# Splitting the qkv weight sums by tile, other interleaving constants, and a last product in two column halves, in a fused attention and GLU kernel on one Trainium2 core

## The chip, the core and the metric

The kernel runs on one core of a Trainium2 chip. The core has a matrix engine (TensorE; PE in the profile for its matmuls, PEld for its weight loads), VectorE (DVE), ScalarE (ACT), GpSimd (POOL) and SyncE (SP), each with its own instruction queue that is worked through in order, and 16 DMA engines that SP, ACT and POOL give transfers to. Matmuls write PSUM, which is divided into eight banks of 128 partitions by 512 f32; everything else lies in SBUF, 128 partitions wide. The metric is the device time of one execution in microseconds.

## What is computed

A sliding-window attention (32 heads of 32, eight keys per query at distances 0, 2, ..., 14) and a gated feed-forward layer work on the same 2048 rows of 1024, and a sigmoid gate per row mixes them. All inputs and outputs are bf16.

```python
def reference(A_x, A_wqkv, A_wo, B_x, B_w_gate, B_w_up, B_w_down, gate_w):
    x = A_x                                                   # 1 x 2048 x 1024
    g = sigmoid((x * gate_w).sum(-1, keepdims=True))
    # attention: q, k, v = x @ wqkv (1024 x 3072); softmax over 8 keys
    #   s, s-2, ..., s-14 of each head; o @ wo (1024 x 1024)
    a = _A_ref(x, A_wqkv, A_wo)
    # feed-forward: (gelu(x @ w_gate) * (x @ w_up)) @ w_down, 1024 -> 3584 -> 1024
    b = _B_ref(x, B_w_gate, B_w_up, B_w_down)
    return g * a + (1 - g) * b
```

## The kernel before, in words

**Tiling.** The rows are worked on in four chunks `c` of 512 (`SC`), in two pairs (`sup` 0: chunks 0 and 1; `sup` 1: chunks 2 and 3). Each large product is done as a 2x2 block product in Strassen's way with seven multiplications instead of eight, for which sums and differences of weight blocks, of activations and of partial results are needed. TensorE does the multiplications as matmuls of 128x128 weights with 512 moving columns. VectorE makes the sums, and with ScalarE it empties the banks.

**Stages of TensorE**, in the order of `main()`: turning the first rows, the q product of the first pair (`first_pair`, L592, and L772), k and v of the first pair (`qkv_pair`, L772), the feed-forward products of the first pair (`ffn`, L1136) with the beginning of the output product of chunk 0 in them (`down`, L1305), the rest of that output product, q, k and v of the second pair (L592, L772; in the order q, v, k, `QVK`), the output product of chunk 1, the feed-forward products of the second pair, and the output products of chunks 2 and 3. The last thing that is computed is the seventh multiplication (`m` = 6) for the second half (`g` = 1) of chunk 3: 18 matmuls into one bank, which ScalarE scales into an SBUF tile (`scaled`, L1346) and SP writes to DRAM (`evac`, L1338).

**VectorE's other work.** In the gaps between the sums it does the attention of all chunks: products of queries and shifted keys (L937) and their additions (L943), the softmax (L1014 to L1060), products with values (L1084) and additions (L1094, L1098, L1102). In the products of q, k and v it empties banks: in `qkv_pair` at L837, by an addition that must be done before the bank's last product (T4, the form `(1, 1)`) may start, and at L847; in `ffn` at L1203 and L1224.

**The weight sums at L709** (`qkv_forms`). For each of q, k and v of a pair, four sums `f` are made, each in two operations `kt` = 0 and 2, and each operation covers two neighbouring weight tiles `kt` and `kt + 1`. The raw tiles (128 x 1024 each) lie, for most of them, in slots of a ring of 20 (`ring`, one slot of 128 x 1024 for each tile); the slots are handed out in the order in which they come free, so two neighbouring tiles need not be neighbours. The operand of an operation is therefore written with the distance between the two slots as its outermost step. `f` = 2 is made in place in the raw tiles; the others take a slot of the ring.

**What sets the order.** `Weave.run` takes operations from eleven streams (main line, loads, sums, preparation of `w_down` and `wo` forms, attention, scores and so on) and issues the one that its own clock thinks can start first. To that start time each stream's bias is added, unless the operation has a due time that is near; an operation may have a bias of its own. The bias of the streams, the due times `DUE`, and the costs of the operations are constants in the source. The order on each engine is fixed when the program is built; waits are by semaphore.

Of the kernel before, what the change touches and what calls it, by code (L numbers as in the profile page):

```python
# [9 lines left out]
ALU = mybir.AluOpType  # L10
# [17 lines left out]
def _win_ap(src: bass.AP, dims):  # L28
    return AP(src.tensor, src.offset, [list(src.ap[0])] + [list(d) for d in dims])
# [125 lines left out]
def kernel(  # L155
# [68 lines left out]
    DUE = (77.1, 303.05)  # L224
# [25 lines left out]
    def dve(cost, fn, deps=(), **kw):  # L250
        return Op("DVE", cost, fn, deps, **kw)
# [211 lines left out]
    def preps():  # L463
        for i0 in range(0, NPREP, 2):
# [5 lines left out]
            f0 = dve(t, lambda: V(out=b11, in0=b12, in1=b11, op=ALU.subtract), due=DUE[0] + 3.05 * i0, deps=[("prep", i0), ], lag=1.0)  # L470
            yield f0
            yield dve(t, lambda: V(out=b12, in0=b22, in1=b12, op=ALU.subtract), due=DUE[0] + 3.05 * i0)
            f1 = dve(t, lambda: V(out=b22, in0=b22, in1=b11, op=ALU.subtract), [f0], due=DUE[0] + 3.05 * i0)
            yield f1
            last = dve(t, lambda: V(out=b21, in0=b21, in1=b22, op=ALU.subtract), [f1], due=DUE[0] + 3.05 * i0)
# [12 lines left out]
    def wforms():  # L488
        t = tt(GR)
        for b in range(NBLK):  # L490
            ops = []
            for f, x_, y_, op in ((0, "U21", "A22", ALU.add), (2, "A11", "U21", ALU.subtract), (1, 0, "A11", ALU.subtract),
                                  (3, "A12", 1, ALU.subtract)):
                def go(f=f, x_=x_, y_=y_, op=op, b=b):
# [4 lines left out]
                        due=DUE[0] + 12.1 * b)  # L499
# [187 lines left out]
    def qkv_forms():  # L687
        for sup in range(NSUP):
            c = 2 * sup
            t = tt(D)  # L690
            for which in QVK if sup else (0, 1, 2):
                def raw(kt, hi, which=which, c=c):
                    w0, w1 = qkv_w(c, which, kt), qkv_w(c, which, kt + 1)
                    return _win_ap(w0[:, KH * hi:KH * hi + 1], [[w1.offset - w0.offset, 2], [NT, P], [1, KH]])

                def form(f, kt, which=which, c=c):
                    return ring[:, held["wqf", c, which, f, kt // 2], :].rearrange("p (k m t) -> p k m t", k=2, t=KH)

                for f in range(4):
                    for kt in range(0, KH, 2):  # L700
                        def go(f=f, kt=kt, which=which, c=c):
# [7 lines left out]
                            V(out=o(), in0=x_(), in1=y_(), op=op)  # L709
# [574 lines left out]
    def down(c):  # L1284
# [5 lines left out]
        def prod(bk, m, g, start, deps):  # L1290
# [7 lines left out]
            for q in range(last + 1):  # L1298
                def fn(q=q):
                    wv = piece(("wd", c, m, q), 2)  # L1300
                    for i in range(2):
                        k = 2 * q + i
                        l, kk = (ops[g][a][0], k) if k < FH else (ops[g][a][1], k - FH)
                        l = l[:, kk // 2, kk % 2, :] if len(l.shape) == 4 else l[:, kk, :]
                        nc.tensor.matmul(banks[bk][:], lhsT=l, rhs=wv[:, i, :], start=(start and k == 0),  # L1305
                                         stop=(q == last and i == 1), skip_group_check=True)
# [3 lines left out]
                if g == 1:  # L1310
                    ring_give(("wd", c, m, q), o)
# [18 lines left out]
    def down_rest(c, prod, ev, A, Bk, Dk, m5, u2, omg, steps):  # L1330
# [4 lines left out]
        def evac(e_op, j, nh, ost):  # L1335
            yield e_op
            yield Op("SP" if last else "POOL", (P * NW * 2, 0.5),
                     lambda: eng.dma_start(out=o2[s0 + j * P:s0 + (j + 1) * P, nh * NW:(nh + 1) * NW], in_=ost[0]),  # L1338
                     [e_op])
# [8 lines left out]
        for m, g in steps:  # L1348
# [3 lines left out]
            if True:  # L1352
# [25 lines left out]
                elif m == 4:  # L1378
# [4 lines left out]
                    yield from evac(ev[g, "x"], j2, 1, box)  # L1383
                elif m == 5:
# [5 lines left out]
                    bank_give(Dk[g], e)  # L1390
                else:
# [7 lines left out]
    def main():  # L1399
# [57 lines left out]
```

## Time and profile before

| What | Value |
|---|---|
| Median of three runs | 722.49 us (722.13 to 722.61) |
| The profiled execution, span from the first to the last instruction | 720.1 us |
| What lies around that span, by the median | 2.4 us |
| Granted TensorE clock over the span | 1.000 |
| DMA moved over the span | 176.84 MB, mean 246 GB/s |
| VectorE busy, 84 to 251 us | 163.3 of 167 us |
| VectorE busy, 251 to 309 us | 51.2 of 58 us |
| VectorE busy, 309 to 344 us | 34.7 of 35 us |
| VectorE busy, 344 to 384 us | 32.5 of 40 us |
| VectorE busy, 384 to 616 us | 211.1 of 232 us |
| L709 in all | 48 operations of 128x1024, 678 to 694 ns each |

The profiled execution's span is measured on the core; a run's time also holds what comes before the first and after the last instruction. In the tables that follow, times are microseconds from the span's start. A line of the timeline gives the start, the length, the engine, the line of the source, the operation, its output and inputs, how many instructions were put together (x), and in square brackets how long the engine had been idle before and what ended that. The length of an operation is from its start to its end; on VectorE and ScalarE the next operation can begin some 0.08 us before that end, when it needs nothing from it. On TensorE the end of a matmul is modelled, and the next one starts well before it: rows of matmuls start 0.216 us apart.

### The profile page before, as it was taken

The numbers are of one execution on the slowest core, as the hardware profiler recorded it, in microseconds if no ns is written. First come the engines' busy times: TensorE is split into PE (matmuls) and PEld (weight loads), VectorE is DVE, ScalarE is ACT, GpSimd is POOL, SyncE is SP. The second block draws the span as 40 slices with busy tenths as digits, with TensorE's granted clock in tenths as the row PEclk, the third lists the DMA queues.
The fourth block names the chain that finished last, engine by engine and source line by source line (L and its number), as shares of the span: only waits on it lengthen the run. The fifth ranks groups of instructions, "written<-read, shape, count | busy, mean of one in ns | idle before, by whom it ended". The sixth has DMA issues, their size and how long they took to land.

```text
span 720.1 us, 9892 instructions
## 1 busy us (share of the span) xinstructions
PE 710.1 (99%) x3337; PEld 342.7 (48%) x3337; DVE 609.8 (85%) x862; ACT 323.8 (45%) x547; POOL 73.8 (10%) x130
## 2 busy tenths in 40 slices
PE   7999999999999999999999999999999999999997
PEld 3556544444444444456554444444444444444443
DVE  4989999999998999799789988799999997849300
ACT  3354585555585522153465323258556655310110
POOL 0020333343121100100000000100000000001000
PEclk9999999999999999999999999999999999999999
DMA  9953899996797799943378899996647656999992
GB/s 263 363 192 97 248 295 311 362 317 225 179 249 230 238 253 330 336 174 117 88 214 272 277 299 352 311 310 186 185 137 194 172 165 161 322 294 376 297 338 93
DMA packets 184179, 176.84 MB, mean 246 GB/s; under 512 B 58304, under 2 KB 140224, under 8 KB 184000
## 3 DMA queue, kind: packets, MB, share of 16 engines
q1 hardware_dynamic: 174512, 145.53, 68.6%
q0 software_dynamic: 9328, 30.42, 11.6%
q8 instruction: 26, 0.43, 0.2%
q10 hardware_dynamic: 288, 0.26, 0.1%
q14 instruction: 25, 0.20, 0.1%
HBM read 132.12 MB, written 31.46 MB: 227 GB/s over the span
## 4 chain that ended last, share of the span: by engine, by line
PE 96%; DVE 1%; SPq 1%; DMA 1%; issue 0%; ACT 0%; DVEq 0%
PE ps L1136 47%; PE ps L1305 30%; PE ps L772 18%; PE ps L592 1%; SPq L357 1%; DMA hT<-in_A_wqkv_dram 1%; DVE ring L709 0%; SPq L428 0%; DVE lend L837 0%; DVE tf L518 0%; DVE zt L880 0%; PE ps L874 0%; ACT ost L1346 0%; DVE hT L709 0%; PE ps L898 0%
## 5 line engine op out<-in xcount | busy, mean ns | idle before, releaser
L1136 PEld LDWEIGHTS <-ring 128*128 128x128 bf16 x1568 | 153.2, 98 | 185.1 <-issue 0.5
L1136 PE MATMUL ps<-lend,ring 128*128 128x512 bf16 x896 | 212.7, 379 | 0.0
L1136 PE MATMUL ps<-tf,ring 128*128 128x512 bf16 x672 | 164.3, 379 | 0.0
L1305 PE MATMUL ps<-ring,hT 128*128 128x512 bf16 x708 | 160.7, 379 | 0.0
L1305 PEld LDWEIGHTS <-hT 128*128 128x128 bf16 x708 | 69.1, 98 | 83.8 <-DVE ost L1380 0.4
L1084 DVE TENSOR_TENSOR xbuf<-xbuf,lend 128x2048 bf16<-128x2048 bf16 x64 | 77.5, 1217 | 16.6 <-DMA xbuf<-xbuf 16.5
L772 PEld LDWEIGHTS <-ring 128*128 128x128 bf16 x512 | 65.0, 127 | 49.6 <-issue 3.6
L937 DVE TENSOR_TENSOR xbuf<-qo,lend 128x2048 bf16<-128x2048 bf16 x64 | 77.0, 1218 | 2.3 <-ACT lend L830 2.3
L943 DVE TENSOR_TENSOR xbuf<-xbuf 128x2048 bf16<-128x2048 bf16 x56 | 68.2, 1218 | 0.2
L772 PE MATMUL ps<-tf,ring 128*128 128x512 bf16 x256 | 58.4, 380 | 3.2 <-DVE lend L837 1.4
L772 PE MATMUL ps<-lend,ring 128*128 128x512 bf16 x256 | 57.9, 379 | 0.0
L1346 ACT ACTIVATE ost<-ps,omg 128x512 bf16<-128x512 f32 x16 | 11.0, 687 | 101.3 <-PE ps L1305 89.7
L1168 ACT COPY ps<-ps 128x512 f32<-128x512 f32 x56 | 32.1, 573 | 51.8 <-PE ps L1136 51.6
L1212 ACT ACTIVATE gl<-ps 128x512 bf16<-128x512 f32 x56 | 33.5, 598 | 46.5 <-PE ps L1136 46.3
L1305 PE MATMUL ps<-ring,qo 128*128 128x512 bf16 x192 | 49.3, 380 | 0.0
L1338 POOL DMA_DIRECT2D out_dram<-ost x24 | 13.0, 541 | 336.6 <-ACT ost L1346 248.3
L1185 DVE TENSOR_TENSOR hT<-hT,gl 128x1024 bf16<-128x1024 bf16 x56 | 38.3, 685 | 8.6 <-ACT hT L1178 8.5
L505 POOL DMA_DIRECT2D fforms<-ring x56 | 30.8, 551 | 144.2 <-DVE ring L496 138.1
L1224 DVE TENSOR_TENSOR u<-ps,u 128x512 f32<-128x512 f32 x56 | 38.3, 685 | 2.7 <-PE ps L1136 2.3
L1228 ACT ACTIVATE gl<-u 128x512 bf16<-128x512 f32 x56 | 35.4, 633 | 11.3 <-DVE u L1224 10.7
L1220 ACT COPY u<-ps 128x512 f32<-128x512 f32 x56 | 32.8, 586 | 14.3 <-PE ps L1136 14.3
L1094 DVE TENSOR_TENSOR xbuf<-xbuf 128x2048 bf16<-128x2048 bf16 x32 | 38.9, 1217 | 0.1
(120 smaller groups left out, 668.8 us busy)
## 6 DMA issues: line engine op xcount, KB each, us to landing
ring<-dforms SPq DMA_DIRECT2D x112, 256.0 KB, 5.0
ring<-in_B_w_down_dram SPq DMA_DIRECT2D x84, 256.0 KB, 5.4
ring<-in_B_w_gate_dram SPq DMA_DIRECT2D x56, 256.0 KB, 5.4
fforms<-ring POOLq DMA_DIRECT2D x56, 256.0 KB, 5.2
ring<-fforms SPq DMA_DIRECT2D x56, 256.0 KB, 4.1
ring<-in_B_w_up_dram SPq DMA_DIRECT2D x42, 256.0 KB, 4.8
ring<-in_A_wqkv_dram SPq DMA_DIRECT2D x32, 256.0 KB, 4.5
ring<-oforms SPq DMA_DIRECT2D x32, 256.0 KB, 5.6
```

What stands on the lines that cost most here:

```text
L772: nc.tensor.matmul(banks[bk][:], lhsT=lhsT, rhs=rhs[:, kt, :], start=(start and kt == 0), stop=(kt == KH - 1), skip_group_check=True)
L937: V(out=w3(box[t]), in0=q_b, in1=k_w, op=ALU.mult)
L943: V(out=w3(box[0]), in0=w3(box[0]), in1=w3(box[t]), op=ALU.add)
L1084: return dve(tt(n), taking(("p", t), lambda: V(out=w3(box["p", t]), in0=w3(box["ab"]), in1=v_w, op=ALU.mult)), [("qkv", c, 2, t), abo] + ( ...
L1094: V(out=p0.rearrange("p (u n) -> p u n", u=2), in0=lo, in1=hi, op=ALU.add)
L1136: nc.tensor.matmul(banks[bk][:], lhsT=wv[:, k, fl * P:(fl + 1) * P], rhs=rhs[:, k, :], start=(start and k == 0), stop=(k == KH - 1), skip_ ...
L1185: yield dve(tt(2 * SC), lambda hv=hv, gv=gv: nc.vector.tensor_tensor(out=hv, in0=hv, in1=gv, op=ALU.mult), [e, ev[f, "g1"], ev[f, "g2"]], ...
L1212: nc.scalar.activation(out=gl[f][:, r1 * SC:(r1 + 1) * SC], in_=banks[A[f]][:], func=ACT.Gelu_apprx_tanh)
L1220: nc.scalar.copy(out=u2[f][:], in_=banks[Bk[f]][:])
L1224: e = dve(tt(SC, True), lambda f=f: nc.vector.tensor_tensor(out=u2[f][:], in0=banks[Dk[f]][:], in1=u2[f][:], op=ALU.add), [o, ev[f, "u2"]])
L1228: ev[f, "g2"] = act(0.54, lambda f=f: nc.scalar.activation(out=gl[f][:, r2 * SC:(r2 + 1) * SC], in_=u2[f][:], func=ACT.Gelu_apprx_tanh), [ ...
L1305: nc.tensor.matmul(banks[bk][:], lhsT=l, rhs=wv[:, i, :], start=(start and k == 0), stop=(q == last and i == 1), skip_group_check=True)
```

## The change

Four things are done.

**The sums at L709.** When the slots of the two tiles are neighbours, an operation stays as it was. Otherwise it is written as two operations, one for each tile, of half the size. This holds for an operation as soon as one of its raw operands lies apart. The planner is told 0.065 us more for each operation whose raw tiles lie in the ring.

**Constants.** The due times of the `w_down` and `wo` preparations, of the feed-forward weight sums and of the qkv sums, the operations' own bias for the first pair's q and k sums, and the bias of five streams.

**The last product.** The multiplication `m` = 6, `g` = 1 of chunk 3 is done as two passes of 18 matmuls with 256 columns each, where it was 18 matmuls with 512. The second pass goes into another bank, into which ScalarE copies the upper 256 columns of the accumulated bank after the fifth multiplication (`m` = 4) has been taken out. Each pass is scaled by ScalarE and written to DRAM by itself.

**The output write** (`evac`) takes a range of columns.

```diff
-    DUE = (77.1, 303.05)
+    DUE = (80.01, 302.59)
...
-            f0 = dve(t, lambda: V(out=b11, in0=b12, in1=b11, op=ALU.subtract), due=DUE[0] + 3.05 * i0, deps=[("prep", i0), ], lag=1.0)
+            f0 = dve(t, lambda: V(out=b11, in0=b12, in1=b11, op=ALU.subtract), due=DUE[0] + 2.82 * i0, deps=[("prep", i0), ], lag=1.0)
...
-                        due=DUE[0] + 12.1 * b)
+                        due=DUE[0] + 11.2 * b)
...
                 def raw(kt, hi, which=which, c=c):
                     w0, w1 = qkv_w(c, which, kt), qkv_w(c, which, kt + 1)
-                    return _win_ap(w0[:, KH * hi:KH * hi + 1], [[w1.offset - w0.offset, 2], [NT, P], [1, KH]])
+                    step = w1.offset - w0.offset
+                    if step == D:
+                        return [_win_ap(w0[:, KH * hi:KH * hi + 1], [[D, 2], [NT, P], [1, KH]])]
+                    return [_win_ap(z[:, KH * hi:KH * hi + 1], [[NT, P], [1, KH]]) for z in (w0, w1)]
...
+                def parts(z, n):
+                    return z if len(z) == n else [z[0][:, k] for k in range(2)]
...
-                            V(out=o(), in0=x_(), in1=y_(), op=op)
+                            args = [z() for z in (o, x_, y_)]
+                            m = max(len(z) for z in args)
+                            for o1, x1, y1 in zip(*[parts(z, m) for z in args]):
+                                V(out=o1, in0=x1, in1=y1, op=op)
...
-                        op = dve(t, go, dep, key=("wq", c, which, f, kt), lag=0.5,
+                        op = dve(t if c < 2 and which != 1 else t + 0.065, go, dep, key=("wq", c, which, f, kt), lag=0.5,
...
-                                 bias=(0.1, -0.6)[which == 0] if which < 2 and not sup else None,
-                                 due=DUE[1] + 23.0 * QVK.index(which) + 2.5 * f if sup else 0.0)
+                                 bias=(0.19, -1.0)[which == 0] if which < 2 and not sup else None,
+                                 due=DUE[1] + 12.84 * QVK.index(which) + 0.09 * f if sup else 0.0)
...
+                    if last and g == 1:
+                        hi, fr = bank_take(True)
+                        ev["hi"] = act(0.3, lambda g=g: nc.scalar.copy(out=banks[hi][:, 0:NW // 2], in_=banks[Bk[g]][:, NW // 2:NW]),
+                                       [ev[g, "x"]] + ([fr] if fr else []), after=True)
+                        yield ev["hi"]
...
+                elif last and g == 1:
+                    hw = NW // 2
+                    o = yield from prod(Bk[g], m, g, False, [ev[g, "x"]], (0, hw))
+                    e = act(0.4, lambda g=g, om2=om2, box=box: nc.scalar.activation(
+                        out=ost_tile(box)[:, 0:hw], in_=banks[Bk[g]][:, 0:hw], func=ACT.Copy, scale=om2), [o])
+                    yield from evac(e, j2, 0, box, 0, hw)
+                    bank_give(Bk[g], e)
+                    o = yield from prod(hi, m, g, False, [ev["hi"]], (hw, NW))
+                    e = act(0.4, lambda om2=om2, box=box: nc.scalar.activation(
+                        out=box[0][:, hw:NW], in_=banks[hi][:, 0:hw], func=ACT.Copy, scale=om2), [o])
+                    yield from evac(e, j2, 0, box, hw, NW)
+                    bank_give(hi, e)
...
-    w.run([(0.0, main()), (0.0, loads()), (0.0, late_x()), (0.0, moves(3)), (0.63, wforms()), (0.0, down_forms()), (0.1, x_forms()), (2.39, qkv_forms()),
-           (2.06, preps()), (0.02, attention()), (0.28, scores())])
+    w.run([(0.0, main()), (0.0, loads()), (0.0, late_x()), (0.0, moves(3)), (0.64, wforms()), (0.0, down_forms()), (0, x_forms()), (2.0, qkv_forms()),
+           (1.54, preps()), (0.1, attention()), (0.28, scores())])
```

`prod` and `evac` get the column range as arguments (`cols`, `o0` and `c0`, `c1`); for all other products they are called as before.

More of the change, by code (lines that the diff above doesn't have):

```diff
@@ L469, in preps @@
             t = tt(n * NW)
-            f0 = dve(t, lambda: V(out=b11, in0=b12, in1=b11, op=ALU.subtract), due=DUE[0] + 3.05 * i0, deps=[("prep", i0), ], lag=1.0)
+            f0 = dve(t, lambda: V(out=b11, in0=b12, in1=b11, op=ALU.subtract), due=DUE[0] + 2.82 * i0, deps=[("prep", i0), ], lag=1.0)
             yield f0
-            yield dve(t, lambda: V(out=b12, in0=b22, in1=b12, op=ALU.subtract), due=DUE[0] + 3.05 * i0)
-            f1 = dve(t, lambda: V(out=b22, in0=b22, in1=b11, op=ALU.subtract), [f0], due=DUE[0] + 3.05 * i0)
+            yield dve(t, lambda: V(out=b12, in0=b22, in1=b12, op=ALU.subtract), due=DUE[0] + 2.82 * i0)
+            f1 = dve(t, lambda: V(out=b22, in0=b22, in1=b11, op=ALU.subtract), [f0], due=DUE[0] + 2.82 * i0)
             yield f1
-            last = dve(t, lambda: V(out=b21, in0=b21, in1=b22, op=ALU.subtract), [f1], due=DUE[0] + 3.05 * i0)
+            last = dve(t, lambda: V(out=b21, in0=b21, in1=b22, op=ALU.subtract), [f1], due=DUE[0] + 2.82 * i0)
             yield last
@@ L693, in raw @@
                     w0, w1 = qkv_w(c, which, kt), qkv_w(c, which, kt + 1)
-                    return _win_ap(w0[:, KH * hi:KH * hi + 1], [[w1.offset - w0.offset, 2], [NT, P], [1, KH]])
+                    step = w1.offset - w0.offset
+                    if step == D:
+                        return [_win_ap(w0[:, KH * hi:KH * hi + 1], [[D, 2], [NT, P], [1, KH]])]
+                    return [_win_ap(z[:, KH * hi:KH * hi + 1], [[NT, P], [1, KH]]) for z in (w0, w1)]
                 def form(f, kt, which=which, c=c):
-                    return ring[:, held["wqf", c, which, f, kt // 2], :].rearrange("p (k m t) -> p k m t", k=2, t=KH)
+                    return [ring[:, held["wqf", c, which, f, kt // 2], :].rearrange("p (k m t) -> p k m t", k=2, t=KH)]
+                def parts(z, n):
+                    return z if len(z) == n else [z[0][:, k] for k in range(2)]
                 for f in range(4):
@@ L1288, in down, with prod @@
         A, Bk, Dk, m5, u2, ev = {}, {}, {}, {}, {}, {}
-        def prod(bk, m, g, start, deps):
+        def prod(bk, m, g, start, deps, cols=(0, NW), o0=0):
             a = SEQ[m][0]
@@ L1304, in fn @@
                         l = l[:, kk // 2, kk % 2, :] if len(l.shape) == 4 else l[:, kk, :]
-                        nc.tensor.matmul(banks[bk][:], lhsT=l, rhs=wv[:, i, :], start=(start and k == 0),
-                                         stop=(q == last and i == 1), skip_group_check=True)
+                        nc.tensor.matmul(banks[bk][:, o0:o0 + cols[1] - cols[0]], lhsT=l, rhs=wv[:, i, cols[0]:cols[1]],
+                                         start=(start and k == 0), stop=(q == last and i == 1), skip_group_check=True)
                 need = [("h", sup, FH + 2 * q + 1)] if (m == 1 and 2 * q < FH) else []
@@ L1309, in prod @@
                 yield o
-                if g == 1:
+                if g == 1 and cols[1] == NW:
                     ring_give(("wd", c, m, q), o)
@@ L1333, in down_rest, with evac @@
         eng = nc.sync if last else nc.gpsimd
-        def evac(e_op, j, nh, ost):
+        def evac(e_op, j, nh, ost, c0=0, c1=NW):
             yield e_op
-            yield Op("SP" if last else "POOL", (P * NW * 2, 0.5),
-                     lambda: eng.dma_start(out=o2[s0 + j * P:s0 + (j + 1) * P, nh * NW:(nh + 1) * NW], in_=ost[0]),
+            yield Op("SP" if last else "POOL", (P * (c1 - c0) * 2, 0.5),
+                     lambda: eng.dma_start(out=o2[s0 + j * P:s0 + (j + 1) * P, nh * NW + c0:nh * NW + c1], in_=ost[0][:, c0:c1]),
                      [e_op])
```

## The prediction

> **What bounds the kernel now.** First the page's busy times and the shares of the chain that ended last.
>
> ```profile
> PE 710.1 (99%) x3337; PEld 342.7 (48%) x3337; DVE 609.8 (85%) x862; ACT 323.8 (45%) x547; POOL 73.8 (10%) x130
> ...
> PE 96%; DVE 1%; SPq 1%; DMA 1%; issue 0%; ACT 0%; DVEq 0%
> ```
>
> TensorE sets the end. Nothing can be won but its waits, its own work and the tail behind it. So next the waits of TensorE (total, times, longest):
>
> ```profile
> PE ps L592 <- DMA hT<-in_A_wqkv_dram: 1.5, 1, 1.5
> PE ps L772 <- DVE lend L837: 1.4, 2, 0.9
> PE ps L772 <- DVE tf L516: 1.0, 1, 1.0
> PE ps L322 <- DVE xbuf L320: 0.9, 1, 0.9
> PE ps L772 <- DVE zt L880: 0.8, 1, 0.8
> PE ps L592 <- ACT lend L559: 0.7, 1, 0.7
> ```
>
> All but L837 fall before 21 us. The two waits for L837, in TensorE's timeline:
>
> ```profile
> 338.21 5.34 PE L772 MATMUL ps<-lend,ring 128*128 128x512 bf16 x24
> 344.50 1.89 PE L772 MATMUL ps<-tf,ring 128*128 128x512 bf16 x8 [0.94 <-DVE lend L837]
> ...
> 363.49 5.34 PE L772 MATMUL ps<-lend,ring 128*128 128x512 bf16 x24
> 369.27 1.89 PE L772 MATMUL ps<-tf,ring 128*128 128x512 bf16 x8 [0.44 <-DVE lend L837]
> ```
>
> The idle time shown is too small for what is lost, since a matmul's modelled end lies after the next one could start. By the start distance (the output products run 468 matmuls in 101.02 us in the chain, 0.216 each), 24 matmuls from 338.21 let the next start at 343.39; it started at 344.50: 1.11 lost. From 363.49: 368.67 against 369.27, 0.60 lost. VectorE's timeline says why L837 is late:
>
> ```profile
> 308.65 5.21 DVE L709 TENSOR_TENSOR ring<-ring 128x1024 bf16<-128x1024 bf16 x8 [1.07 <-DMA ring<-in_A_wqkv_dram]
> 313.78 1.22 DVE L1084 TENSOR_TENSOR xbuf<-xbuf,lend 128x2048 bf16<-128x2048 bf16 x1
> ...
> 339.10 2.35 DVE L937 TENSOR_TENSOR xbuf<-qo,lend 128x2048 bf16<-128x2048 bf16 x2
> 341.37 2.48 DVE L943 TENSOR_TENSOR xbuf<-xbuf 128x2048 bf16<-128x2048 bf16 x2
> 343.76 1.28 DVE L837 TENSOR_TENSOR lend<-ps,m5q 128x512 bf16<-128x512 f32 x2
> ...
> 366.40 2.22 DVE L1266 TENSOR_TENSOR hT<-hT 128x1792 bf16<-128x1792 bf16 x2 [2.75 <-DMA parked<-hT]
> 368.54 1.28 DVE L837 TENSOR_TENSOR lend<-ps,m5q 128x512 bf16<-128x512 f32 x2
> ```
>
> The first time VectorE was busy without a gap from 308.65 on, with four attention operations just ahead of L837. The second time L837 stands behind L1266, which waits for the store of parked rows, a transfer. Last, the tail:
>
> ```profile
> 712.35 3.19 PE L1305 MATMUL ps<-ring,hT 128*128 128x512 bf16 x14
> 715.37 1.03 PE L1305 MATMUL ps<-ring,qo 128*128 128x512 bf16 x4
> 716.44 0.69 ACT L1346 ACTIVATE ost<-ps,omg 128x512 bf16<-128x512 f32 x1 [3.20 <-PE ps L1305]
> ```
>
> After it come the write (1.7 us to landing, least and median of the last five) and the closing waits, up to 720.1.
>
> **The change, part by part.** I read the changed order of each engine off its built program. TensorE's order is the same up to the last product; so are ScalarE's instructions, but for the new ones and table loads in other places, which leave it 45% busy.
>
> *First L837 wait.* Of the scores, one L937 and one L943 now stand before 303 us, where VectorE idles (1.23 at 301.29 behind L1305, 1.91 at 303.95 behind a transfer), and no longer between the second group of sums and L837. Start to start they took 1.13 and 1.25: L837 comes 2.38 earlier. Against this: (a) one L1094 (1.13) moves behind the first sum. That sum waited 1.07 for loads; as halves, each with its own tiles' loads to wait for, they may start sooner, so between 0 and 1.13 is added. (b) 15 of the 16 operations in the two groups ahead are split. A run of eight took 5.13 (308.65 to 313.78), 0.64 each; of a half-size operation (L1102, 128x512 bf16, 0.42 long) the next start follows after 0.34, so a pair costs 0.68: +0.04 each, 0.6. Sum: 343.76 - 2.38 + 0.60 gives 341.98, with (a) in full 343.11. To cost TensorE nothing L837 must start by about 343.39 - 0.69 = 342.7. So 1.11 is won at the one end, 0.7 at the other. I take 1.0; the bound below is 0, if the loads of these sums come a microsecond later (see the second rival).
>
> *Second L837 wait.* The order there is the same, and the store that is waited for is issued when ScalarE has emptied q's and v's banks, that is on TensorE's time: if all comes 1 us earlier, so does this. SP gives six loads at 359 to 363 us that compete with it. The three stores of this kind took 5.3, 6.9 and 8.6 us (least, median, most); 0.6 less would end the wait. Bounds 0 and 0.60; I take 0.1, near the unchanged row.
>
> *Splits in all.* 25 operations become 50 (2 for the first pair, 23 for the second). VectorE pays 25 x 0.04 = 1.0 us, at most 25 x (2 x 0.418 - 0.685) = 3.8. Off TensorE's path I price it at nothing; the cover is VectorE's idle time in 344 to 384 us (7.5 us) and 2.75 of waiting ahead of L1266. With that gone it would reach L837 at 368 and cost up to 8 x 0.15 = 1.2 (the eight splits of the third group).
>
> *First pair.* Two in-place sums now run ahead of L516, which so starts 0.6 later, and its product starts at 17.1 instead of 16.5. But the sums (0.6) are missing again before 18.7, and TensorE waits at 20.76 for L880, whose place is kept: 0. The cover is that wait, 0.8. L602's second copy moves behind the first sum and ends at about 12.6, when its matmul is due: perhaps 0.1, in the same cover.
>
> *Queues.* On SP one transposed load of the rows of chunk 3 goes ahead of two loads of `wo` and another behind one load of forms. Each such issue takes 1.27 (four in 5.07 at 251.41), so the loads behind come up to 1.3 later. No wait of TensorE for a ring load appears from 21 us on, so nothing; without that reserve 1.3. The read-back of the parked values goes three loads later, long before its use. POOL's stores of sums are regrouped; POOL is 10% busy: 0.
>
> *The last product.* 36 matmuls of 256 columns instead of 18 of 512. No row has 256 columns. The rows beside it:
>
> ```profile
> 4.31 0.90 PEld L550 LDWEIGHTS <-hT 128*128 128x128 bf16 x16 [0.69 <-DMA hT<-in_A_x_dram]
> 4.31 1.07 PE L550 MATMUL ps<-hT 128*128 128x128 bf16 x16
> ```
>
> 16 loads and matmuls with 128 columns follow each other at 56 ns (0.90/16), 512 columns at 216. On the line between, 256 takes 109: 36 x 109 = 3.93 against 18 x 216 = 3.89, +0.05. Upper bound: a load takes 98 ns in the groups; were none hidden, 36 x 0.098 = +3.5. Lower: 0. The 128-column row hides them, so +0.05.
>
> The Trainium skill ("TensorE: Matmul & The Clock Gate", section "LDWEIGHTS (loading the stationary operand)") gives a load of 128 columns about 107 ns, as long as 256 moving columns take, so that a split of columns leaves a load no room. Were loads and matmuls to take turns, the sum by it would be 36 x 0.107 = 3.9 us worse; the 56 ns row speaks against it.
>
> ScalarE's last operation has half the width: 0.687 at 512, 0.206 at 4 columns (L1041), so 0.445 at 256: -0.24 (bounds 0 and -0.34). The copy into the other bank runs in ScalarE's idle time, and the first half's scaling and write pass under the second pass (1.96 us). The last write is 64 KB instead of 128: between 0 and half of its 1.7, and I take -0.15, since the 64 KB saved are 0.27 at the mean rate of 246 GB/s, and the rest of the write isn't size. The closing waits of SP go through the transfer semaphores in turn; with one write more the last stands one place later: -0.06.
>
> *Sum:* -1.0 - 0.1 + 0.05 - 0.24 - 0.15 - 0.06 = -1.5. The profiled execution, 720.1, becomes 718.6; the median, 2.4 above it, 722.49 - 1.5 = **721.0**. Its own range 720.4 to 721.6.
>
> **The rivals.**
>
> *Both L837 waits go.* The store lands 0.6 sooner, because the loads from 359 us now follow sums that end later by their splits. For it: the spread of the stores; against: the order. 721.0 - 0.5 = 720.5.
>
> *The first wait stays and the change doesn't do what it says.* L1094 in full, and the loads of these sums 0.8 later from the moved transposes: 343.11 + 0.8 is 343.9, later than now. Then only the tail is won: 722.49 - 0.5 = 722.0.
>
> *VectorE becomes the bound in the first feed-forward stage (84 to 251 us): slower.* It is busy 163.3 of 167 there, and the sums, preparations and attention come in another order throughout. About 203 us an L496, an L943, another L496 and a whole chain of softmax operations stand between an L1224 and the L1203 that empties a bank. From 196.68 (L1224) these are 0.60 + 0.60 + 1.13 + 0.60 + 1.04 + 0.59 + 0.26 + 0.33, then L1185 0.60 and L1203 0.69: 203.1, and the bank's next matmul started at 203.3. There, 0.2 is left. A sum that waits for its load, as at 218.83 for 0.86, would cost 0.7. From four such places on (2.8 - 1.5 = +1.3, about the bound of slower) it decides; with five 722.49 + 2.0 = 724.5. Against it: TensorE doesn't wait once between 21 and 343 us now, with the same work.
>
> **How the numbers follow.** About 0.2%, 1.44 us, is what a measurement of this kernel can tell from no change: faster is under 721.05, slower over 723.93. Forecast 0.58; as its middle lies at the bound, 0.33 faster, 0.25 same. Both waits gone 0.16, faster. First wait stays 0.13, same. VectorE bound 0.13, slower. Together 0.49, 0.38 and 0.13. Range 720.4 to 722.4, which leaves out the slower case and the upper end of the third.
>
> **What would show it.** L837 gone from TensorE's waits near 343 us, one left near 368; no new VectorE or transfer line among the waits between 21 and 343; matmuls of 256 columns about 0.11 apart; a last ScalarE operation of some 0.45; VectorE some 1 us busier at L709's line between 300 and 362. It is wrong if TensorE waits in the feed-forward stage or at ring loads, if the 256-column matmuls are over 0.15 apart, or if L837 at 343 still begins after its bank is needed.

## The result, and the profile after

The changed kernel takes 724.23 us (median of 12 runs, 722.92 to 725.36) beside 722.70 (12 runs on the same chip, 722.13 to 723.74): ratio 1.0019, 95% interval 1.0011 to 1.0027, slower by some 1.5 us. Ratios here compare undisturbed runs alone and medians take all, so a ratio need not be the quotient of two medians.

The profiled execution of the changed kernel took 723.86 us with a span of 722.1: 1.8 us lie around the span, as in all 12 runs with the span beside the time (1.73 to 1.84). So the execution of before with the span of 720.1 must have taken about 721.9 us, 0.8 under that kernel's median, and the two spans lie 2.0 apart where the medians lie 1.5 apart. The spans are used for where the time went, the medians for how much. Lines after the change stand nine lower in the source from L718 on: the sums L709 are now L718, L837 is L846, L1136 is L1145, L1203 is L1212, L1224 is L1233, L1305 is L1314; L470 to L516 are unchanged. So L1203 of after is L1194 of before, and not the L1203 named there. Kernels with an edit in `loads` stand three lower still from there on.

Lost time of TensorE, counted as in the prediction by the distance from start to start:

| Where | Predicted | Before | After | Difference |
|---|---|---|---|---|
| up to 33 us | 0 | | | +0.11 |
| at 141 us | 0 | 0 | 1.45 | +1.45 |
| at 168 and twice at 203 to 205 us | 0 | 0 | 0.66 | +0.66 |
| first L837 wait, 343 us | -1.0 | 1.11 | 0.01 | -1.10 |
| second L837 wait, 369 us | -0.1 | 0.60 | 1.98 | +1.38 |
| two waits of 0.17 at 381 and 392 us | | 0.34 | 0.06 | -0.28 |
| tail | -0.40 | | | -0.30 |
| sum | -1.5 | | | +1.9 |

The trace has the spans to the hundredth, 720.13 and 722.09: they lie 1.96 apart.

First, the busy times and the shares of the chain that ended last, after:

```profile
PE 706.8 (98%) x3289; PEld 344.2 (48%) x3355; DVE 610.5 (85%) x887; ACT 323.6 (45%) x549; POOL 73.8 (10%) x130
...
PE 81%; issue 10%; DVE 4%; DMA 3%; SPq 1%; POOL 1%; ACT 0%; DVEq 0%; POOLq 0%
```

The program has 18 matmuls more than before and as many weight loads as matmuls, 3355. That the page counts 3289 matmuls, 48 fewer than before, means that 66 records are missing. That is also how the chain gets its 10% of "issue": it loses TensorE where records are missing and goes on along another engine. Neither the busy time of PE nor the chain's shares can be compared between the two kernels. VectorE is busy 0.7 us longer, and its rows of sums alone grew by 1.5 (31.4 to 32.9). What can be compared is the waits of TensorE:

```profile
PE ps L592 <- DMA hT<-in_A_wqkv_dram: 1.8, 1, 1.8
PE ps L781 <- DVE lend L846: 1.8, 1, 1.8
PE ps L781 <- DVE tf L516: 1.4, 1, 1.4
PE ps L1145 <- ACT m L1203: 1.3, 1, 1.3
...
PE ps L781 <- DVE zt L889: 0.2, 1, 0.2
```

L846 waits once instead of twice, and longer than both waits of before together (1.4). A new line stands at L1145, in the first feed-forward stage, where before there was none. The first, third and last line belong to the first 21 us, where the later L516 is taken off the wait for L889, as the prediction said; the wait for L592 is 0.3 longer, of which it had nothing, and +0.11 is left. The new wait, in the timeline of after:

```profile
139.14 0.69 DVE L472 TENSOR_TENSOR hT<-hT 128x1024 bf16<-128x1024 bf16 x1 [2.03 <-DMA hT<-in_B_w_down_dram]
139.75 0.68 DVE L496 TENSOR_TENSOR ring<-ring 128x1024 bf16<-128x1024 bf16 x1
140.35 0.69 DVE L1233 TENSOR_TENSOR u<-ps,u 128x512 f32<-128x512 f32 x1
...
141.07 0.63 ACT L1237 ACTIVATE gl<-u 128x512 bf16<-128x512 f32 x1 [3.29 <-DVE u L1233]
...
142.07 0.59 ACT L1203 COPY m<-ps 128x512 f32<-128x512 f32 x1
...
142.71 1.46 PE L1145 MATMUL ps<-lend,ring 128*128 128x512 bf16 x6 [1.28 <-ACT m L1203]
```

Read from the top: VectorE stands 2.03 us at L472, a preparation of `w_down` forms, whose load has not landed. L496 and L1233 stand behind it. ScalarE has been waiting for L1233 for 3.29 us, does L1237 and what follows, and comes late to L1203, the copy that empties a bank for TensorE. TensorE needs nothing of L472 here (`preps_later`, below, runs it 1.64 us later); it costs because VectorE works in order. Now L846, in VectorE's timeline:

```profile
344.35 1.28 DVE L846 TENSOR_TENSOR lend<-ps,m5q 128x512 bf16<-128x512 f32 x2
...
368.93 2.22 DVE L1275 TENSOR_TENSOR hT<-hT 128x1792 bf16<-128x1792 bf16 x2 [3.77 <-DMA parked<-hT]
371.06 1.28 DVE L846 TENSOR_TENSOR lend<-ps,m5q 128x512 bf16<-128x512 f32 x2
```

By 343 us TensorE is 2.3 us later than before, so L846 at 344.35 is in time; what the moved scores and the halves did for that can't be told from this execution. At L1275 the wait for the store of parked rows grew from 2.75 to 3.77 us: the store takes 8.30 us from its issue to its landing, 6.92 before. Last, the tail:

```profile
716.57 1.69 PE L1314 MATMUL ps<-ring,hT 128*128 128x256 bf16 x14
...
718.10 0.60 PE L1314 MATMUL ps<-ring,qo 128*128 128x256 bf16 x4
718.73 0.47 ACT L1413 ACTIVATE ost<-ps,omg 128x256 bf16<-128x256 f32 x1 [1.49 <-PE ps L1314]
```

14 matmuls from 716.57 to 718.10 are 0.109 us each, as drawn on the line between 56 ns and 216. ScalarE's half takes 0.47 instead of 0.69.

### The profile page after: what moved, and what is told of

Same layout as the page of the kernel before. It is cut to its first block, busy times and chain, and to the rows that moved or that the text cites. A ratio compares the mean times of both kernels' runs of the same rounds, so it can differ in the third digit from the quotient of the medians.

```text
span 722.1 us, 9900 instructions
## 1 busy us (share of the span) xinstructions
PE 706.8 (98%) x3289; PEld 344.2 (48%) x3355; DVE 610.5 (85%) x887; ACT 323.6 (45%) x549; POOL 73.8 (10%) x130
## 4 chain that ended last, share of the span: by engine, by line
PE 81%; issue 10%; DVE 4%; DMA 3%; SPq 1%; POOL 1%; ACT 0%; DVEq 0%; POOLq 0%
PE ps L1145 45%; PE ps L1314 26%; PE ps L781 10%; DMA parked<-hT 1%; DMA ring<-dforms 1%; DMA ring<-in_B_w_down_dram 1%; SPq L357 1%; DMA hT<-in_A_wqkv_dram 1%; POOL out_dram L1347 0%; DVE ring L496 0%; DVE ring L718 0%; DVE u L1233 0%; DVE xbuf L1038 0%; DVE zt L889 0%; DVE hT L1212 0%
## 5 line engine op out<-in xcount | busy, mean ns | idle before, releaser
L1145 PEld LDWEIGHTS <-ring 128*128 128x128 bf16 x1568 | 153.3, 98 | 187.1 <-issue 2.8
L1145 PE MATMUL ps<-lend,ring 128*128 128x512 bf16 x879 | 210.9, 379 | 2.2 <-ACT m L1203 1.3
L1145 PE MATMUL ps<-tf,ring 128*128 128x512 bf16 x658 | 162.7, 379 | 0.9
L1314 PE MATMUL ps<-ring,hT 128*128 128x512 bf16 (+1 forms) x706 | 159.8, 375 | 0.8
L1314 PEld LDWEIGHTS <-hT 128*128 128x128 bf16 x722 | 70.6, 98 | 82.6 <-DVE xbuf L952 0.4
L1314 PE MATMUL ps<-ring,qo 128*128 128x512 bf16 (+1 forms) x192 | 49.1, 375 | 0.2
L1237 ACT ACTIVATE gl<-u 128x512 bf16<-128x512 f32 x56 | 35.4, 632 | 26.1 <-DVE u L1233 25.7
L1194 DVE TENSOR_TENSOR hT<-hT,gl 128x1024 bf16<-128x1024 bf16 x56 | 38.6, 689 | 9.7 <-ACT hT L1187 9.6
L1233 DVE TENSOR_TENSOR u<-ps,u 128x512 f32<-128x512 f32 x56 | 38.6, 689 | 2.4 <-PE ps L1145 2.3
L1103 DVE TENSOR_TENSOR xbuf<-xbuf 128x2048 bf16<-128x2048 bf16 x32 | 39.1, 1222 | 0.0
L1212 DVE TENSOR_TENSOR hT<-ps,m 128x512 bf16<-128x512 f32 x56 | 38.6, 689 | 0.3 <-PE ps L1145 0.2
```

Of the source, the lines that this page charges most:

```text
L1103: V(out=p0.rearrange("p (u n) -> p u n", u=2), in0=lo, in1=hi, op=ALU.add)
L1145: nc.tensor.matmul(banks[bk][:], lhsT=wv[:, k, fl * P:(fl + 1) * P], rhs=rhs[:, k, :], start=(start and k == 0), stop=(k == KH - 1), skip_ ...
L1194: yield dve(tt(2 * SC), lambda hv=hv, gv=gv: nc.vector.tensor_tensor(out=hv, in0=hv, in1=gv, op=ALU.mult), [e, ev[f, "g1"], ev[f, "g2"]], ...
L1212: ev[f, "up2"] = dve(tt(SC, True), lambda f=f: nc.vector.tensor_tensor(out=hs(f, 1), in0=v3(banks[Bk[f]][:]), in1=v3(m5[f][:]), op=ALU.add ...
L1233: e = dve(tt(SC, True), lambda f=f: nc.vector.tensor_tensor(out=u2[f][:], in0=banks[Dk[f]][:], in1=u2[f][:], op=ALU.add), [o, ev[f, "u2"]])
L1237: ev[f, "g2"] = act(0.54, lambda f=f: nc.scalar.activation(out=gl[f][:, r2 * SC:(r2 + 1) * SC], in_=u2[f][:], func=ACT.Gelu_apprx_tanh), [ ...
```

## The experiments

All are built on the changed kernel and were timed in five rounds. "Lost" is the time TensorE lost in the profiled execution at 141 to 207, 343 and 369 us; before has 0, 1.11 and 0.60, after 2.11 (1.45 of it at 141), 0 and 1.98.

### The tail alone

`tail_only`: the last product and `evac` as changed, all else as before.

```diff
-    DUE = (80.01, 302.59)
+    DUE = (77.1, 303.05)
...
-                    if step == D:
-                        return [_win_ap(w0[:, KH * hi:KH * hi + 1], [[D, 2], [NT, P], [1, KH]])]
-                    return [_win_ap(z[:, KH * hi:KH * hi + 1], [[NT, P], [1, KH]]) for z in (w0, w1)]
+                    return [_win_ap(w0[:, KH * hi:KH * hi + 1], [[step, 2], [NT, P], [1, KH]])]
```

(and the other constants.)

> The kernel before with the last product in two 256-column passes and nothing else changed. From the trace of the changed kernel: the first of the last matmuls to the start of the last ScalarE operation took 4.13 us against 4.09, that operation 0.47 against 0.69, and the rest of the span behind it 2.9 against 2.97, so 0.25 us less in all: 722.45 against 722.7, a ratio of 0.9997. By the prediction's own terms (+0.05 -0.24 -0.15 -0.06) it would be 0.40 less, 722.3. If the second pass costs TensorE more in other executions (loads not hidden, 0.15 us apart), it is 1.4 us more, 724.1. The waits at 343 (1.1) and 368 us (0.6) stay as in the kernel before under all of these.

Measured: 722.26 us beside 722.85, ratio 0.9993 (0.9985 to 1.0002); lost 0, 1.20 and 0.39. By the spans to the hundredth (719.91 here) the tail is 0.32 us shorter than in the profile of before, and 0.30 in after. By terms: +0.04 for the matmuls, -0.21 for ScalarE, and -0.15 (in after -0.13) for what lies behind ScalarE's end, the write and the closing waits together. A write of 64 KB landed in 1.6 us, one of 128 KB in 1.7. The gain stands in both profiles and is too small for the interval.

### The first feed-forward stage: splits or order?

`merged_cost` keeps the changed kernel's planner, so every engine gets its order, but writes each split sum as one operation again (the same `raw` as in `tail_only`).

> The changed kernel with every sum as one operation over both tiles again; the order on every engine stays that of the changed kernel. Theory (the splits free the feed-forward loads too early): a sum over two tiles that lie apart covers the slots between them too, so the first three of the six loads at 357 us wait for VectorE again, the store of the parked rows lands in about 7 us instead of 8.3, and TensorE's wait at 369 falls from 1.98 to 0.6 or less; the stall of 1.45 at 141 us, where nothing is split, stays. 724.2 - 1.4 = 722.8. First rival (the store's time spreads by itself): 369 stays near 2.0, 724.2. Second rival (the splits' longer VectorE time is what costs): the stalls at 141 to 207 us (2.1) go as well, 720.7. The wait at 343: gone if the moved scores were enough, back by up to 1.1 if it takes the halves.

Measured: 722.72 beside 722.85, ratio 0.9989 (0.9976 to 1.0002); lost 2.21 (1.55 at 141), 0.38 and 0.19. The wait at 141 is there without a single split: it is not theirs.

`ffn_order` keeps the splits and gives the operations of some 76 to 272 us the order of before. `ORDER` is a list with the stream of each operation; the clock chooses nothing any more.

```diff
-            for s in live:
+            for s in [z for z in live if z[3] == int(ORDER[len(self.log)], 16)]:
```

> The changed kernel, but the operations between about 76 and 272 us are issued in the order of the kernel before (an order written out by hand); the rest keeps the changed kernel's order, the splits and the two passes. Theory (the new order in the first feed-forward stage is what stalls TensorE at 141, 168, 203 and 207 us): these 2.14 us go, 724.2 - 2.1 = 722.1; the wait at 343 stays gone, the one at 369 stays near 2.0. Rival (these stalls come from the changed earlier stage, so from ring slots and loads that stand elsewhere, or from the spread of the transfers): they stay, 724.2.

Measured: 722.18 beside 722.85, ratio 0.9990 (0.9981 to 0.9999); lost 0, 0 and 1.48. With the order of before the stage loses nothing again, so the new constants are the cause, by the order they make.

The same edit in two parts was to say where. `ffn_order_a` takes the order of before from 76 to 114 us only, `ffn_order_b` from 114 to 272 only.

> The changed kernel with the order of the kernel before for the operations between about 76 and 114 us only, so that the scores stand behind the weight sums there. Theory (the stall at 141 us has its root in the softmax that ends late at 108 us): the stall of 1.45 at 141 us goes, the 0.7 at 168 to 207 us stay: 722.8. Rival (its root is the order around 141 us itself): it stays, 724.2.

> The changed kernel with the order of the kernel before for the operations between about 114 and 272 us only. Theory (as for the run with the order of 76 to 114 us): the stall at 141 us stays, between 0.4 and 1.55 as in the runs so far, and the 0.7 at 168 to 207 us go: 723.5. Rival (the order around 141 us itself): both go, 722.1.

Measured: `ffn_order_a` 723.68 beside 722.64, ratio 1.0011 (0.9998 to 1.0024), lost 2.47 (1.83 at 135 us and 0.64 later), 0 and 2.29. `ffn_order_b` 722.96 beside 722.64, ratio 1.0005 (0.9991 to 1.0019), lost 0.36, 0 and 1.82. My theory was that the scores which now run at 76 to 82 us delay the softmax of 103 us, with it the transpose on SP (issued at 107.3 us, 104.1 before) and the loads behind that. In `ffn_order_a` that transpose was on time again, and the wait only moved: L496 stood 2.79 us at 133.97 for a ring load. In the profiles the order from 114 us on decides, the rival's answer; the times don't tell the two kernels apart, their intervals overlap.

`trans_behind` tested the queue itself: the transpose of 107.3 us goes behind the eight loads that followed it on SP.

> The changed kernel with one instruction moved: on SP's queue the attention transpose at 107.3 us (L1084) is issued behind the eight loads that follow it, instead of ahead of them; VectorE's order and all else stay. Theory (that transpose waits for VectorE's softmax, which the new order ends 3 us later, and holds the loads of w_down behind it in SP's queue; their preparation L472 then waits for them on VectorE, and the bank's emptying behind L472): the four loads are issued by about 105 instead of 112 us, L472's waits of 1.4 and 2.0 us go and with them TensorE's stall of 1.45 at 141 us; those of 0.7 in all at 168 to 207 us stay: 724.2 - 1.45 = 722.8. Rival (the DMA engines are full then, and the loads land as late wherever they stand in the queue): the stall stays, 724.2.

Measured: 729.97 beside 722.64, ratio 1.0103 (1.0078 to 1.0127), with 6.61 us lost at 136.1 alone. The expectation failed. SP's own timeline and VectorE's:

```profile
110.83 12.79 SPq L1084 DMA_TRANSPOSE xbuf<-xbuf  x2
```

```profile
139.71 0.69 DVE L496 TENSOR_TENSOR ring<-ring 128x1024 bf16<-128x1024 bf16 x1 [4.27 <-DMA ring<-in_B_w_up_dram]
```

Two transposes now followed each other and held SP for 12.79 us, and every load behind them came later still. The loads were moved out of one wait into a longer one. TensorE stood still for 6.45 us, and behind that the granted clock was 0.50 from 142 to 148 us: 16 matmuls from 142.68 to 148.93 took 6.25 us where 3.45 are usual, which is another 2.8 lost.

`preps_later` asks only who stands at the wrong place: the preparations L472 and L473 go behind the next L1194 in VectorE's order (two entries of `ORDER` moved), and nothing else is changed.

> The changed kernel with two instructions moved on VectorE's queue: L472 and L473 of the preparation whose w_down tiles land at 134 to 138 us stand behind L496, L1233, L1103 and L1194 there, instead of ahead of L496 and L1233 (L472) and between them and L1103 (L473). No queue of transfers changes. Theory (the new constants put this preparation at 136.4 us, where the kernel before has it at 140.2, and its loads land at 138.4 instead of 132.4, so L472 waits with the bank's emptying L1233 behind it): L1233 starts at about 137 us, TensorE's stall of 1.45 at 141 us goes, the 0.7 at 168 to 207 us stay, 724.2 - 1.45 = 722.8 at most, and the profile shows no wait of TensorE for L1203 over 0.4 us near 141. Rival (all loads land late there, and the next instruction that needs one, an L496, stalls in its place, as when the order of 76 to 114 us was put back): a stall of 1 us or more stays between 130 and 150 us, 724.2.

Measured: 722.51 beside 722.77, ratio 0.9990 (0.9978 to 1.0002); lost 0.43 (at 202 to 204), 0 and 1.75. VectorE's timeline:

```profile
138.32 0.68 DVE L1233 TENSOR_TENSOR u<-ps,u 128x512 f32<-128x512 f32 x1
...
140.78 0.68 DVE L472 TENSOR_TENSOR hT<-hT 128x1024 bf16<-128x1024 bf16 x1
```

L1233 runs two microseconds earlier than in after, L472 1.64 later and finds its data there. The wait at 141 is gone, and the times agree: 0.9990 (0.9978 to 1.0002) where after had 1.0019 (1.0011 to 1.0027). So the chain read from the profile of after holds: the loss comes from a preparation ahead of L1233. Its size varies: executions with the same order up to there lost 1.45 (after), 1.55 (`merged_cost`) and 0.39 (`hold_sum`, below, where the same L472 waited 1.12 us).

`stores_later` asked why the load was late: four stores of prepared forms that GpSimd issues at 112 to 115 us (120.7 to 123.6 before) go behind the second store of feed-forward sums.

> The changed kernel with one group moved on GpSimd's queue: the four stores of prepared w_down blocks (L480) that it issues at 112.0 to 115.0 us, between the two attention transposes of SP at 107.3 and 116.8 us, are issued behind the second store of feed-forward sums that follows, from about 121 us, where the kernel before issued them (120.7 to 123.6). VectorE's and SP's orders stay. Theory (DMA engines are full from 110 to 140 us in every run; the preparations, which the new constants put earlier, send their 1 MB of stores ahead of the second transpose and the loads behind it, which so land 4 to 6 us later; L472 waits for them): L472's waits of 1.4 and 2.0 us shrink to under 0.5 in all, TensorE's stall of 1.45 at 141 us goes: 724.2 - 1.45 = 722.8. Rival (VectorE's order alone: L472 stands too early in it for any load): the stall stays, 724.2.

Measured: 721.80 beside 722.79, ratio 0.9990 (0.9980 to 1.0001); but its profiled execution, 723.86, still lost 2.30 (1.65 at 141.6), 0 and 1.44. The `w_down` loads went out 2.5 us earlier in it than in after (122.6 us for 125.1) and the last landed at 138.2, for 138.4. Eight of the twelve runs lie at 721.2 to 722.1, four at 722.85 to 724.0, so the wait may have become rarer: the ratio and its interval lie below those of after. The profile shows one execution only, and this stays open.

### The wait at 369 us: who holds the store?

In after, SP gives the DMA engines six loads (L400) from 357.50 us on, and GpSimd issues the store at 360.54. In before, SP gives its first at 359.34 and GpSimd its store at 359.39. What SP had waited for is in its list of waits, of before and then of `merged_cost` (total, times, longest):

```profile
SPq L400 <- DVE ring L709: 9.0, 1, 9.0
```

```profile
SPq L400 <- DVE ring L718: 9.9, 2, 9.1
```

After has no such line. My reading is that a sum over two slots that lie apart counts, when the program orders its accesses, as one access to the whole stretch from the one to the other, and so to the slots between too. The loads into those must wait until VectorE is through. By the waits this held the first of the six in before, the first two in `merged_cost` and none with the halves; SP works in order and held the others behind. `merged_cost` has the order of after, so it is the split that took these waits away, and the loads went ahead of the store.

`hold_sum` puts one of them back: the first of the six loads waits for the last qkv sum, and SP, working in order, holds the rest behind it. The order of after is written out in `ORDER`.

```diff
-            yield ring_load(("w", sup, b, name), lambda g, v=v: nc.sync.dma_start(
+            o = ring_load(("w", sup, b, name), lambda g, v=v: nc.sync.dma_start(
...
+            if (sup, b, name) == (1, 0, "A11"):
+                o.after, o.deps = True, list(first)
+            yield o
```

> The changed kernel, order and splits as they are, with one wait added: the first of the six feed-forward loads at 357 us waits for the last sum of the qkv weights, about 362.6 us, so that all six stand behind the store of the parked rows at 360.5. Theory (these loads, 3 us ahead of the store, delay it): the store lands in 5.3 to 7 us, TensorE's wait at 369 falls from 1.98 to between 0 and 0.6: 724.2 - 1.4 to 2.0 = 722.2 to 722.8. Rival (the store's time spreads by itself): it stays, 724.2. If the loads, now 5 us later, are missing at the start of the second feed-forward stage, a new wait at 385 to 400 us of up to 1 us takes part of it back.

Measured: 722.33 beside 722.85, ratio 0.9984 (0.9974 to 0.9994); lost 1.05 (0.39 at 141), 0 and 0. SP's first load, and VectorE:

```profile
361.81 0.38 SPq L400 DMA_DIRECT2D ring<-in_B_w_gate_dram  x1
```

```profile
365.54 2.22 DVE L1278 TENSOR_TENSOR hT<-hT 128x1792 bf16<-128x1792 bf16 x2 [1.23 <-ACT xbuf L1078]
367.67 1.28 DVE L849 TENSOR_TENSOR lend<-ps,m5q 128x512 bf16<-128x512 f32 x2
```

The load goes out 2.12 us after the store (issued at 359.69), which lands in 5.75, at 365.44. L1278 (L1275 in after) starts 0.10 later, where the profile names ScalarE as what it waited for last, and L849 (L846) is in time. One wait put back wins more than what before itself lost there. The cleanest pair is further below: `best2` is `ffn_order` with this wait and nothing else, 0.9968 (0.9955 to 0.9980) for 0.9990 (0.9981 to 0.9999). Over all runs:

| Loads given ahead of the store | Store, issue to landing |
|---|---|
| none (`hold_sum`, `best`, `best2`) | 5.75 to 5.77 us |
| one (before, `tail_only`, `merged_cost`) | 6.50 to 6.92 |
| two (`ffn_merged`) | 8.03 |
| six (after and six variants of its order) | 7.75 to 8.61 |

The Trainium skill ("DMA: Bandwidth & Descriptors", section "Issuing engines are not separate DMA queues") says that transfers run on the same 16 DMA engines whichever engine started them. The table agrees: a store on GpSimd's queue pays for the loads on SP's.

### The wait at 343 us: are the halves needed?

The prediction put the gain on two score operations moved away. `ffn_merged` has the order of `ffn_order` and whole sums.

> The run with the order of the kernel before from 76 to 272 us, but with every sum as one operation over both tiles. TensorE is then on time at 343 us, so this tells what the two scores that were moved ahead do without the halves. Prediction's step (the moved scores give 2.38, the halves cost 0.6, the attention operation moved behind the first sum up to 1.13): without halves L837's successor starts 0.6 earlier still and the wait at 343 stays gone; at 368 us the loads are held by VectorE again, so 0.6 or less is lost: ratio to the kernel before about 0.998, 721.3. Rival (a whole sum waits for the loads of four tiles and more slots, so the groups start later): the wait at 343 is back by up to 1.1, 722.4.

Measured: 722.82 beside 722.79, ratio 0.9998 (0.9989 to 1.0007); lost 0, 1.14 and 1.71. VectorE of `ffn_merged`, then of `ffn_order`:

```profile
309.89 0.70 DVE L718 TENSOR_TENSOR ring<-ring 128x1024 bf16<-128x1024 bf16 x1 [3.47 <-DMA ring<-in_A_wqkv_dram]
...
311.64 4.67 DVE L718 TENSOR_TENSOR ring<-ring 128x1024 bf16<-128x1024 bf16 x7
...
343.96 1.28 DVE L846 TENSOR_TENSOR lend<-ps,m5q 128x512 bf16<-128x512 f32 x2
```

```profile
306.88 0.42 DVE L718 TENSOR_TENSOR ring<-ring 128x512 bf16<-128x512 bf16 x1
...
309.50 4.78 DVE L718 TENSOR_TENSOR ring<-ring 128x512 bf16<-128x512 bf16 x14
...
342.22 1.28 DVE L846 TENSOR_TENSOR lend<-ps,m5q 128x512 bf16<-128x512 f32 x2
```

The whole sum starts 0.12 us after the last of the loads it needs has landed (309.77). The halves start with their own tiles, and the L1103 that stands behind them (L1094 of before, the operation of (a) in the prediction) is done while the other loads are still on their way. So the run of sums behind starts 2.1 us earlier in `ffn_order`. Not all of that is the halves: the last of these loads landed at 309.22 there, 0.55 earlier. My estimate for the halves is the remaining 1.6 us. In `ffn_merged` the move of the scores won nothing. The 342.22 lies inside the 341.98 to 343.11 of the prediction. At 369 us the theory's 0.6 was missed: in this order the slots fall differently, only the second and the fourth load wait for VectorE, and two go ahead of the store.

### Putting the good parts together

`best`: splits and tail of the change, its order from 272 us on, the order of before up to there, and the held load. `best2`: the same with the changed order in the first 76 us.

> The order of the kernel before up to 272 us, the changed kernel's order, splits and two passes from there on, and the first of the six feed-forward loads at 357 us held behind the last qkv sum. By the theory what the change lost is gone and what it won stays: against the kernel before -1.1 (wait at 343 us), -0.6 (wait at 368 us), -0.25 (tail) and up to -0.3 (small waits at 381 and 392 us) make 722.7 - 2.0 to 2.2 = 720.5 to 720.7, a ratio of 0.997. If the halves' longer VectorE time or the held loads cost elsewhere, it is 722 or more.

> As the run with the order of the kernel before up to 272 us and the held loads, which measured 720.4 and still lost 1.14 us at 343 us in its profile, but with the changed kernel's first 76 us. If that loss came from the order of the first 76 us (other ring slots for the second pair's loads), it goes here: 720.4 - 1.1 = 719.3; if it comes and goes with the landing of the transfers at 305 us, the median stays near 720.4, and this profile may or may not show it.

Measured: `best` 720.37 beside 722.64, ratio 0.9966 (0.9954 to 0.9978); lost 0, 1.14 and 0. `best2` 720.42 beside 722.79, ratio 0.9968 (0.9955 to 0.9980); lost 0, 1.10 and 0, and 0.92 behind 469 us. Both are faster than before by some 2.3 us, though the wait at 343 us is back. VectorE of `best2`:

```profile
309.81 0.43 DVE L721 TENSOR_TENSOR ring<-ring 128x512 bf16<-128x512 bf16 x1 [1.67 <-issue]
311.29 4.79 DVE L721 TENSOR_TENSOR ring<-ring 128x512 bf16<-128x512 bf16 x14
```

Of the five kernels with halves in which TensorE had lost under 0.5 us before, three lost nothing at 343 us (`ffn_order`, `ffn_order_b`, `preps_later`) and two lost all (`best`, `best2`). What separates them is when a load lands. `best2` has the order of `ffn_order` throughout and differs in the held load only (355.41 us in `ffn_order`), so up to there the two are the same program. But the load that the second half needs landed at 309.74 in the one execution (issued at 303.88) and at 307.94 in the other (303.09), and that half started at 309.81 and 308.02. In all five L846 (L849) starts 32.7 us after the run of 14 halves; that run starts at 309.50, 310.42 and 309.50 in the three, and at 311.22 and 311.29 in the two. The attention operation ahead of the first half doesn't separate them: it starts at 305.42 in `preps_later` and at 305.45 in `best2`.

So the wait at 343 us can come and go between executions of one program, and each profile shows one: that of `best2` is the slowest of five runs (721.85), that of `ffn_order` the fastest of eleven (721.26). How often the wait is there I do not know.

## Why the prediction was wrong, point by point

**The step that failed first: "No wait of TensorE for a ring load appears from 21 us on, so nothing", and the first feed-forward stage at nothing in the sum.** It measured +2.11. The prediction looked for a wait of TensorE itself, and named as cover that there had been none. But the order from 84 to 251 us was new, on an engine that was busy 163.3 of 167 us. A load that reaches VectorE late reaches TensorE too, through a sum or a preparation that has nothing to do with the bank. `merged_cost` and `ffn_order` show that the order alone makes the loss, `preps_later` that two operations make most of it. Why the loads land late is only partly known: they were issued at 125 to 128 us and landed at 134 to 138, 119 to 122 and 129 to 132 before, in a stretch where the DMA engines are busy for 90% or more (the page's slices from 108 to 162 us). By the times both changes were needed: the preparation's first operation stands at 136.41 us in after and at 140.24 in before, and the last of its loads in the trace landed at 138.4 and at 132.4. Taking the transpose out of their way failed twice. Moving the stores left the wait in its profile, though the run times fell; "POOL's stores regrouped: 0" is thus neither shown right nor refuted.

**The third rival** had this stage and this direction, at 0.13, and its 724.5 lies 0.3 from the measured time. Its mechanism was only half right. It counted some 0.7 at each of four or five places like the one at 203 us; near that one 0.47 was lost in two places, and the most, 1.45, at one place at 141 us, where a preparation and not a sum waited. Its argument against itself, that TensorE did not wait there before "with the same work", was the weak one: the same work in another order is not the same.

**The second step that failed: "Second L837 wait. The order there is the same", with bounds 0 and 0.60.** The bounds held no loss, and it measured +1.38. The prediction itself had the six loads that compete with the store, and the spread of 5.3 to 8.6 us for such stores, but took the loads' times as given. The split removed what held them. `hold_sum` shows it by putting one wait back: 0 lost. The first rival ("both waits go", since the loads follow sums that end later) had the sign wrong for the same reason.

**Right in its number:** the first L837 wait, -1.10 for -1.0. The profile of after doesn't show that it is by the route named, since TensorE was 2.3 us late there; `ffn_order`, with TensorE on time, lost nothing either. In the route one term was mis-sized: the earlier start of the halves stood only in the bounds of (a), and is worth some 1.6 us by the estimate above, without which `ffn_merged` lost 1.14. The bound of nothing was rightly kept, with the condition it had, loads of these sums that come a microsecond later: in `best2` the load landed 1.8 us later than in `ffn_order`, and 1.10 was lost.

**The price of a split** was read too low. In after the starts of two halves lie 0.335 us apart, a pair 0.67; whole sums that follow each other without waiting start 0.60 apart. The 0.64 of the prediction is a run of eight with two short gaps in it (starts 0.73 and 0.78 apart). So a split costs 0.07 and not 0.04, 25 of them 1.7 for the 1.0 said; the rows of the sums grew by 1.5. None of the waits of TensorE in after is put down to it.

**The tail:** -0.30 for -0.40. The passes (+0.04 for +0.05) and ScalarE (-0.21 for -0.24) held. What lies behind ScalarE's end gave -0.13 for -0.21: the write of 64 KB landed 0.1 us sooner than that of 128 KB, for -0.15, and little is left for the closing waits, for -0.06. The 64 KB less are not worth the 0.27 us that the mean rate gave. The load time that the Trainium skill gives ("TensorE: Matmul & The Clock Gate", section "LDWEIGHTS (loading the stationary operand)") would have cost 3.9 us if loads and matmuls took turns, as the prediction weighed; the 256-column matmuls started 0.109 us apart with a load for each, and the 56 ns row was the better guide.

**In sum:** -1.5 became +2.0 in the profiled execution and +1.5 in the medians. The difference of 3.5 is 2.11 of the first stage and 1.48 of the second wait; what remains (+0.11 early, +0.10 in the tail, -0.10 at 343 us, -0.28 in the two small waits) comes to about -0.2.

## What to carry to other kernels

An operation that is planned earlier on an in-order engine needs its transfer earlier too: look up when that transfer lands and who stands behind the operation, above all an operation that empties a bank, even if nothing needs its own result soon. And an edit that removes a dependency lets everything go that the dependency held: ask what starts earlier, and which transfer on the path it then runs into; a wait that looks like waste may be keeping a queue clear.

## What the runs showed of the hardware

A store of parked rows took 5.8 us from issue to landing with no load ahead of it and up to 8.6 with six ahead, though the loads are issued from another engine's queue; with one load 0.03 to 0.05 us ahead of it and the others behind it, it took 6.5 to 6.9. Two transposes from SBUF to SBUF issued back to back held SP for 12.79 us where the pairs near 366 us took 3.15 to 5.56. In the stretch from 115 to 130 us of that run the DMA engines moved 167 to 235 GB/s. In the same run, after TensorE had stood still for 6.45 us, the granted clock was 0.50 from 142 to 148 us, and matmuls of 512 columns started up to 0.43 us apart instead of 0.216.
